# Block-local attention with a squared-ReLU network behind it: the normalisation on VectorE, block means by DMA, and twenty unread products on TensorE

## The chip, the cores and the metric

The kernel runs on one core of a Trainium2 chip. The metric is the device time of one execution in microseconds (us). The core's engines are TensorE (PE, with its weight loads as PEld), VectorE (DVE), ScalarE (ACT), GpSimd (POOL) and SyncE (SP, which here issues every DMA).

## The reference

Attention with B = 4, H = 8, S = 768, D = 64: each query sees the keys closer than 16 positions and, beside them, 24 block keys (the maximum of k over 32 positions, with log 32 added to their scores) whose values are the means of v over the same blocks. The result goes through a network of 512 to 2048 to 512 with a squared ReLU, without bias.

```python
k_sum = k.reshape(B, H, nb, block, D).max(axis=3)
v_sum = v.reshape(B, H, nb, block, D).mean(axis=3)
scores_s = scale * einsum('bhsd,bhnd->bhsn', q, k_sum) + log(block)
scores_l_m = where(|i - j| < window, scale * q @ k.T, -1e9)
a = softmax(concat([scores_l_m, scores_s]))
x = a @ concat([v, v_sum])
out = maximum(x @ w_in, 0) ** 2 @ w_out
```

All in float32 (the weights come as float64).

## The kernel before

**Attention.** The 3072 queries are 48 groups of 64 (group g = 12 b + w), all 8 heads of a group at once. A group's keys are 24 block keys and the 94 around it, 118 in all. The steps of a group, with the task names of the planner: QL loads q; LV loads the local rows of v to partitions 24 to 119 of the group's v tile (line 449, 96 rows of 2 KB), LS puts the 24 rows of block means ahead of them (line 452 a DMA, line 455 a copy on POOL for the first EARLY = 8 groups); S makes the scores (486), X the negated maxima (557, 561), E four exponentials with their sums on ACT (573), R the reciprocals (585, 586), N the product that normalises, on POOL (592), T the transpose (604 on PE for the first eight groups, 621 on DVE with a trip through HBM for the others), A its copy (611), V the product with v (648), XH and XL the high part and the rest of the result (700, 703). For the first eight groups XH is on DVE, for the others, which go in pairs, on ACT. The masks of the first eight groups are added by PE with a second product in S. For groups from 8 on a masking instruction M on DVE (541) does that.

**Per batch.** KL loads k in four pieces of 384 KB and KM takes block maxima on DVE (361). FV loads v in six pieces of 256 KB (405), VM makes means of them on PE (415, three tasks), VS copies the result from PSUM to the tile vs (427, on ACT). KC, a copy on POOL (496), moves the block keys ahead of the next group's local keys in the tile kb, so it has to come between two groups' scores.

**Network.** Six units of 512 tokens (eight groups), 16 slices f of 128 hidden columns. FI makes h = x w_in (813; twelve products of 512 columns: high by high, high by rest, rest by high), RL, SQ, GH, GL (822, 824 or 828, 830, 833) make the square and its two parts, FO adds to the four token blocks of o (843, again twelve products). In the first unit the slices 0 and 1 are split into halves a and b of four groups: h_0a, h_1a, h_0b, h_1b, and their FO likewise. During the first unit the weights are still being converted: WL loads half a slice (747, 512 KB), WM, WH on ACT (750, 764), WR, WJ, WW on DVE (753, 759, 767). PC copies o out (881).

**Order.** The program's order on each engine is the planner's. A task has an engine, a cost, a key (its due time), what it must follow, buffers that it takes, and for a load its size and an earliest time `begin`. `Plan.order()` plays the tasks through with these costs, starts on each free engine the ready task with the lowest key, and the instructions are written out in the order of the starts. So costs, keys, the load rate DMA_RATE and the list FIRST set the order on all engines, but no time on the chip: there each engine takes its list in order and waits by semaphores. SP issues its DMAs in order too.

## Time and profile before

| | |
|---|---|
| median of 3 runs | 635.62 us (635.41 to 636.62) |
| profiled execution | 635.87 us, its span 634.2 us |
| PE busy | 613.0 us, 97% of the span |
| DVE, ACT, POOL busy | 299.6, 268.7, 78.1 us |
| DMA, mean over the span | 116 GB/s |

The span runs from the first to the last instruction, so 1.7 us of the profiled execution lie outside of it. Busy time counts an engine's instructions, without issue and waits. In views of waits, idle time stands beside what ended it. A timeline row may hold several like instructions, with one start and their time together.

### The profile page before, as it was taken

How to read it: one execution, taken by the hardware profiler on the slowest of the kernel's cores; microseconds unless marked ns; L12 is line 12 of the kernel's file. 1: busy time of each engine (PE TensorE's matmuls, PEld its weight loads, DVE VectorE, ACT ScalarE, POOL GpSimd, SP SyncE). 2: the span in 40 equal slices, each digit the busy share in tenths (PEclk: the TensorE clock that was granted, in tenths of full speed). 3: DMA queues.
4: the chain of work that ended last, by engine and by line, in shares of the span. 5: the costliest groups of instructions: out<-in, count | busy, mean ns of one | idle time of the engine just before them, and what ended most of it. 6: DMA issues, size and time to landing. Idle time of an engine off the chain costs nothing.

```text
span 634.2 us, 11015 instructions
## 1 busy us (share of the span) xinstructions
PE 613.0 (97%) x4216; PEld 489.4 (77%) x4216; DVE 299.6 (47%) x517; ACT 268.7 (42%) x709; POOL 78.1 (12%) x140
## 2 busy tenths in 40 slices
PE   4779999999999999999999999999999999999997
PEld 3568788778777778777878778778788788888885
DVE  3798979633433433533543644534444432322221
ACT  1888778626544444332432523414343322222221
POOL 4731101101110110101210101201011010000000
PEclk9999999999999999999999999999999999999999
DMA  8998986244324832232415543133323020100001
GB/s 273 257 310 253 357 313 199 91 108 133 92 60 95 280 86 98 67 84 68 104 48 165 171 132 90 48 85 87 103 72 98 16 67 0 68 0 1 1 1 66
DMA packets 55448, 73.65 MB, mean 116 GB/s; under 512 B 6476, under 2 KB 33100, under 8 KB 55396
## 3 DMA queue, kind: packets, MB, share of 16 engines
q1 hardware_dynamic: 55396, 72.95, 39.0%
q8 instruction: 33, 0.54, 0.4%
q14 instruction: 19, 0.16, 0.1%
HBM read 55.56 MB, written 16.78 MB: 114 GB/s over the span
## 4 chain that ended last, share of the span: by engine, by line
PE 92%; DMA 7%; SPq 0%; DVE 0%; ACT 0%; issue 0%; DVEq 0%
PE o L843 42%; PE h L813 42%; PE x L648 3%; PE att L486 3%; DMA qvpa_lent<-qW 3%; DMA raw<-wW 2%; DMA q<-qW 1%; PE vps L415 1%; SPq L358 0%; PE h_0b L813 0%; PE h_1b L813 0%; DVE os L881 0%; ACT os L881 0%; DVE xl L703 0%; SPq L442 0%
## 5 line engine op out<-in xcount | busy, mean ns | idle before, releaser
L813 PE MATMUL h<-xh,w 128*128 128x512 f32 x752 | 236.9, 396 | 0.0
L843 PE MATMUL o<-w,gh 128*128 128x512 f32 x752 | 196.1, 395 | 1.4 <-DVE os L881 0.8
L843 PEld LDWEIGHTS o<-w,gh 128*128 128x128 f32 x752 | 139.7, 188 | 36.6 <-issue 2.7
L813 PEld LDWEIGHTS h<-xh,w 128*128 128x128 f32 x752 | 140.7, 188 | 33.8 <-issue 0.8
L813 PE MATMUL h<-xl,w 128*128 128x512 f32 x376 | 148.8, 396 | 0.0
L822 ACT ACTIVATE r<-h 128x512 f32<-128x512 f32 x94 | 56.2, 598 | 205.9 <-PE h L813 205.6
L833 DVE TENSOR_TENSOR gl<-r,gh 128x512 fp32r<-128x512 f32 x94 | 66.6, 709 | 101.6 <-ACT gh L830 65.5
L828 DVE TENSOR_TENSOR r<-r 128x512 f32<-128x512 f32 x64 | 45.2, 706 | 139.8 <-ACT r L822 139.7
L843 PE MATMUL o<-w,gl 128*128 128x512 f32 x376 | 106.4, 391 | 0.0
L813 PEld LDWEIGHTS h<-xl,w 128*128 128x128 f32 x376 | 70.6, 188 | 16.9
L843 PEld LDWEIGHTS o<-w,gl 128*128 128x128 f32 x376 | 70.6, 188 | 15.7
L830 ACT CAST gh<-r 128x512 fp32r<-128x512 f32 x94 | 58.3, 620 | 54.1 <-DVE r L828 27.8
L573 ACT ACTIVATE p<-p,nm 128x118 f32<-128x118 f32 x160 | 60.9, 383 | 30.8 <-DVE nm L557 30.7
L592 POOL TENSOR_TENSOR p<-p,nm 128x472 f32<-128x472 f32 x40 | 42.6, 1064 | 114.3 <-DVE nm L586 91.5
L496 POOL COPY kb<-kb 128x96 f32<-128x96 f32 x44 | 16.2, 368 | 306.1 <-PE att L486 282.7
L541 DVE SCALAR_TENSOR_TENSOR p<-att,mask 128x472 f32<-128x472 f32 x38 | 23.5, 644 | 27.8 <-PE att L486 27.8
L621 DVE STREAM_TRANSPOSE a<-p 128x512 f32<-128x512 f32 x40 | 28.3, 707 | 10.4 <-POOL p L592 9.0
L573 ACT ACTIVATION_READ_ACCUMULATOR p<-p,nm 128x1 f32 x160 | 30.0, 187 | 0.0
L557 DVE TENSOR_REDUCE nm<-p 128x4 f32<-128x472 f32 x40 | 25.0, 634 | 0.2
L486 PE MATMUL att<-kb,q 64*64 64x118 f32 x608 | 24.1, 274 | 0.0
L700 ACT CAST xh<-x 128x512 fp32r<-128x512 f32 x20 | 11.6, 582 | 28.6 <-PE x L648 28.6
L759 DVE SCALAR_TENSOR_TENSOR t<-t,raw 128x1024 uint32<-128x1024 uint32 (+1 forms) x19 | 21.8, 1148 | 3.5 <-ACT t L750 3.1
(104 smaller groups left out, 370.9 us busy)
## 6 DMA issues: line engine op xcount, KB each, us to landing
raw<-wW SPq DMA_DIRECT2D x32, 512.0 KB, 6.5
turn<-a SPq DMA_DIRECT2D x160, 64.0 KB, 1.8
a<-turn SPq DMA_DIRECT2D x40, 256.0 KB, 2.7
...
```

What stands on the lines that cost most here:

```text
L486: nc.tensor.matmul(score_tile(g)[c * TQ : (c + 1) * TQ, j, :], lhsT=q_bufs[g].tile[rows, p, :] if term else unscale[rows, :], rhs=kb[rows, ...
L541: nc.vector.scalar_tensor_tensor(out=pr.tile[:, js, :KEYS], in0=score_tile(g)[:, js], scalar=SCALE, in1=mask_of(g)[0].unsqueeze(1).broadca ...
L557: nc.vector.tensor_reduce(out=m, in_=score_tile(g)[:, js] if by_pe else pr.tile[:, js, :KEYS], op=ALU.max, axis=AX.X, negate=True)
L573: nc.scalar.activation(x, score_tile(g)[:, p] if by_pe else x, AF.Exp, bias=nm.tile[:, p : p + 1], scale=SCALE if by_pe else 1.0, accum_ou ...
L592: nc.gpsimd.tensor_tensor(out=x, in0=x, in1=nm.tile[:, 2 * NPAIR :].unsqueeze(2).broadcast_to([P, NPAIR, KEYS]), op=ALU.mult)
L621: nc.vector.transpose(out=a.tile.rearrange("p (j n r) -> p j n r", j=NSQ, n=NPAIR), in_=pr.tile.rearrange("p n (j c) -> p j n c", c=SQ),)
L813: nc.tensor.matmul(cut(h), lhsT=lhs.tile[:, k * P : (k + 1) * P], rhs=rhs[:, k, c0 : c0 + n], start=(i == 0), stop=(i == 3 * KT - 1),)
L822: t2 = add(f"RL{name}", "ACT", act, lambda: nc.scalar.activation(cut(r), cut(h), AF.Relu), due + 3, [t1], take=[r], use=[h])
L828: lambda: nc.vector.tensor_tensor(out=cut(r), in0=cut(r), in1=cut(r), op=ALU.mult), due + 4, [t2], use=[r],
L830: t4 = add(f"GH{name}", "ACT", act, lambda: nc.scalar.copy(out=cut(gh), in_=cut(r)), due + 5, [t3], take=[gh], use=[r])
L833: lambda: nc.vector.tensor_tensor(out=cut(gl), in0=cut(r), in1=cut(gh).bitcast(F32), op=ALU.subtract),
L843: nc.tensor.matmul(o_of(o, t), lhsT=terms[i][0].tile[:, (t - t0) * P : (t - t0 + 1) * P], rhs=terms[i][1].tile, start=(first and i == 0), ...
```

## The change

Line numbers in the diff are those of the changed kernel, which has 1033 lines against 981.

1. N, the normalising product, goes from POOL to DVE for all 48 groups.
2. XH of the first eight groups goes from DVE to ACT, VS of the first batch from ACT to DVE.
3. LS is a DMA for groups from 2 on (before: from 8 on). Two POOL copies are left.
4. LV of the first EARLY + NV = 11 groups reads a new input vF, filled on the host with the same rows of v in place and zeros elsewhere: 128 rows of 2 KB from partition 0, where 96 (or 94) rows went before.
5. Twenty products of the identity with itself (float32, 128 by 128) go into h buffers that nobody reads. They have the last priority on PE: the planner puts one wherever PE would pause. The planner's places are 11 before the first scores, 7 between the two halves of group 0's scores, one behind the first means and one behind the first transpose.
6. The planner's numbers: DMA_RATE, T0 (due time of the first network slice), the due times B0, B1 of groups 4 to 7, FIRST, the earliest `begin` of all other loads (16 instead of 8), and nearly all costs. Hence every engine's order is another.

```diff
-    HOP, DMA_LATENCY, DMA_RATE = 0.12, 1.9, 300e3
+    HOP, DMA_LATENCY, DMA_RATE = 0.12, 1.9, 370e3
...
-    T0, SLOW, STEP, LEAD = 33.0, 6.6, 6.0, 1.5
-    A0, A1, B0, B1 = 14.0, 2.2, 31.0, 2.6
+    T0, SLOW, STEP, LEAD = 29.0, 6.6, 6.0, 1.5
+    A0, A1, B0, B1 = 14.0, 2.2, 23.0, 2.2
...
-        "QL0 KL0_0 KL0_1 KL0_2 KL0_3 QL1 QL2 FV0_0 FV0_1 FV0_2 FV0_3 FV0_4 FV0_5 QL3 LV0 LV1 QL4 WL0_0 LV2 QL5 LV3 "
-        "QL6 LV4 QL7 LV5 WL0_1 LV6 LV7 WL1_0"
+        "QL0 KL0_0 KL0_1 KL0_2 KL0_3 QL1 QL2 FV0_0 FV0_1 FV0_2 FV0_3 FV0_4 FV0_5 QL3 LV0 LV1 QL4 LV2 QL5 LV3 "
+        "QL6 QL7 LV4 LV5 WL0_0 LV6 LV7"
...
+    def warm(i):
+        x = h_buf(f"warm{i}", P)
+
+        def mm():
+            nc.tensor.matmul(x.tile, lhsT=ident, rhs=ident, start=True, stop=True)
+
+        add(f"Y{i}", "PE", 0.42 if i < COLD else 0.22, mm, 1000 + i, [t_ident], take=[x])
+
+    for i in range(WARM):
+        warm(i)
...
-                nc.scalar.copy(out=vs.tile[:, c * P : (c + 1) * P], in_=out_ps.tile[c * SQ : c * SQ + NB, :P])
+                copy(out=vs.tile[:, c * P : (c + 1) * P], in_=out_ps.tile[c * SQ : c * SQ + NB, :P])
+
+        copy = nc.scalar.copy if b else nc.vector.tensor_copy
...
         def load_v():
+            if g < vF.shape[0]:
+
+                nc.sync.dma_start(out=vv.tile, in_=vF[g])
+                return
...
-            if not early:
-                lv.append(add(f"LS{g}", "SP", 0.45, load_s, due - 19, ts + lv, use=[vv, vs_bufs[b]], size=4 * NB * DM))
+            if g >= COPIED:
+                key = FIRST_LS + g if early else due - 19
+                lv.append(add(f"LS{g}", "SP", 0.45, load_s, key, ts + lv, use=[vv, vs_bufs[b]], size=4 * NB * DM))
...
-            nc.gpsimd.tensor_tensor(
+            nc.vector.tensor_tensor(
                 out=x, in0=x, in1=nm.tile[:, 2 * NPAIR :].unsqueeze(2).broadcast_to([P, NPAIR, KEYS]), op=ALU.mult
             )
...
-            (nc.vector.tensor_copy if n == 1 else nc.scalar.copy)(out=by_group(xh), in_=x_all())
+            (nc.vector.tensor_copy if g < HIGH_DVE else nc.scalar.copy)(out=by_group(xh), in_=x_all())
...
-            t.begin = max(t.begin, 8.0)
+            t.begin = max(t.begin, 16.0)
```

COPIED is 2, WARM 20, HIGH_DVE 0. A branch with ONE_EXP = 0 is never taken.

Three places of the order follow. In them, a number behind a name counts buffers, nm holds a group's maxima and sums, qvpa_lent and p are the tiles that hold its exponentials, raw, t and w are steps of a weight's conversion.

On DVE, at groups 3 and 4 of the first stage, there stood before (XH is line 700, XL 703):

```order
L557 TENSOR_REDUCE nm_394<-s_362 128x4
L561 TENSOR_SCALAR nm_394<-nm_394 128x4
L700 CAST xh<-att 128x4x64
L585 TENSOR_SCALAR nm_341<-nm_341 128x4
L586 RECIPROCAL nm_341<-nm_341 128x4
L703 TENSOR_TENSOR xl<-att,xh 128x4x64
L759 SCALAR_TENSOR_TENSOR t_0_405<-t_0_405,raw_0_172 128x512
```

Behind each reciprocal DVE went on without an N, since that was POOL's. With the change DVE has, at groups 4 to 6 (N is line 638):

```order
L798 TENSOR_SCALAR raw_0_276<-raw_0_276 128x512
L638 TENSOR_TENSOR qvpa_lent<-qvpa_lent,nm_411 128x4x118
L583 TENSOR_REDUCE nm_503<-s_464 128x4
L587 TENSOR_SCALAR nm_503<-nm_503 128x4
L631 TENSOR_SCALAR nm_453<-nm_453 128x4
L632 RECIPROCAL nm_453<-nm_453 128x4
L804 SCALAR_TENSOR_TENSOR t_0_508<-t_0_508,raw_0_276 128x512
L638 TENSOR_TENSOR qvpa_lent<-qvpa_lent,nm_453 128x4x118
```

Each group's N moved in between the group's reciprocals and the maxima of the group two later, and XH is gone from the list.

On PE, at slice 4 of the first unit, there stood before (415 is VM; gh_2 and gl_2 are the inputs of the FO of slice 2):

```order
L813 MATMUL h_4_886<-xl,w_860 128x512
L486 MATMUL att<-kb,q_281 64x118 x8
L648 MATMUL x_908<-a_729,v_75 64x64 x8
L648 MATMUL x_908<-a_791,v_76 64x64 x8
L486 MATMUL att<-kb,q_603 64x118 x8
L415 MATMUL vps_955<-fv_0_863,means 24x128 x8
L843 MATMUL o_0_709<-w_2_828,gh_2_866 128x512 x4
L843 MATMUL o_1_830<-w_2_828,gh_2_866 128x512 x4
L843 MATMUL o_0_709<-w_2_828,gl_2_882 128x512 x2
L843 MATMUL o_1_830<-w_2_828,gl_2_882 128x512 x2
L415 MATMUL vps_955<-fv_2_884,means 24x128 x8
L813 MATMUL h_5_1009<-xh,w_905 128x512 x2
```

FO stood two slices behind FI here. With the change PE has at this place (434 is VM, 888 is FO):

```order
L858 MATMUL h_4_987<-xl,w_908 128x512
L434 MATMUL vps_1017<-fv_0_935,means 24x128 x8
L888 MATMUL o_0_798<-w_844,gh_3_943 128x512 x4
L888 MATMUL o_1_864<-w_844,gh_3_943 128x512 x4
L888 MATMUL o_0_798<-w_844,gl_3_979 128x512 x2
L888 MATMUL o_1_864<-w_844,gl_3_979 128x512 x2
L858 MATMUL h_5_1065<-xh,w_940 128x512 x2
```

Behind the FI of slice 4 now comes the FO of slice 3: FO follows its FI one slice closer. The second and third VM both moved behind the FI of slice 5 (one stood ahead of it), so one more FO comes ahead of them.

On SP, at the loads of the second batch, there stood before (405 is FV, 358 is KL, 449 is LV):

```order
L405 DMA fv_0_863<-vS 128x512
L747 DMA raw_876<-wW 128x512 x2
L405 DMA fv_2_884<-vS 128x512 x2
L405 DMA fv_4_948<-vS 128x512 x2
L747 DMA raw_953<-wW 128x512
L442 DMA q_966<-qW 128x256
L449 DMA v_75<-vS 64x512
L449 DMA v_75<-vS 30x512
L358 DMA kb<-kT 128x768 x4
```

All FV came ahead of the loads of k. With the change SP has at this place (424 is FV, 377 is KL, 473 is LV):

```order
L424 DMA fv_0_935<-vS 128x512 x2
L424 DMA fv_2_985<-vS 128x512
L462 DMA q_1001<-qW 128x256
L473 DMA v_75<-vS 64x512
L473 DMA v_75<-vS 30x512
L377 DMA kb<-kT 128x768 x4
L424 DMA fv_2_985<-vS 128x512
L462 DMA q_1029<-qW 128x256
L424 DMA fv_4_1047<-vS 128x512 x2
L473 DMA v_76<-vS 96x512
```

The last three of the six FV moved behind the batch's four loads of k.

## Rows read from the trace of the kernel before

**Rows 1.** Waits of PE over the whole span: engine, line, releaser: us, times, longest.
```profile
PE s L486 <- DVE kb L361: 7.2, 3, 5.5
...
PE s L486 <- POOL kb L496: 0.6, 1, 0.6
```

**Rows 2.** Windows: length, busy us (x instructions) by engine, clock, DMA share, GB/s.
```profile
12.00:26.00 14.00, 12.45 (x272) 9.26 (x264) 8.75 (x25) 10.30 (x49) 8.50 (x18) 1.00 1.07 242
26.00:50.50 24.50, 18.48 (x253) 15.31 (x254) 23.89 (x54) 20.87 (x69) 11.59 (x16) 1.00 1.01 305
50.50:54.00 3.50, 3.50 (x16) 2.81 (x16) 3.50 (x7) 2.28 (x5) 0.00 (x0) 1.00 0.49 146
54.00:100.00 46.00, 46.00 (x347) 36.11 (x346) 40.03 (x52) 35.45 (x69) 2.77 (x5) 1.00 0.93 313
13.00:28.00 15.00, 12.79 (x293) 9.75 (x289) 9.95 (x29) 11.60 (x54) 9.89 (x17) 1.00 1.07 233
```

**Rows 3.** Timeline of PE: start us, us, instruction, idle before it and releaser.
```profile
10.76 0.46 PE L486 MATMUL s<-kb,qvpa_lent 64*64 64x118 f32 x2 [0.40 <-DVE kb L361]
...
13.19 0.62 PE L486 MATMUL s<-mask,unscale 64*64 64x118 f32 x8
...
15.39 0.38 PE L486 MATMUL s<-mask,unscale 64*64 64x118 f32 x8
...
46.25 0.39 PE L813 MATMUL h_0b<-xl,w 128*128 128x256 f32 x1 [1.05 <-DVE xl L703]
...
50.34 0.63 PE L813 MATMUL h<-xh,w 128*128 128x512 f32 x2
...
70.92 0.64 PE L415 MATMUL vps<-fv,means 128*24 128x128 f32 x16
...
74.36 0.62 PE L813 MATMUL h<-xh,w 128*128 128x512 f32 x2
...
77.16 2.02 PE L843 MATMUL o<-w,gh 128*128 128x512 f32 x8
```

**Rows 4.** Timeline of DVE, same columns.
```profile
20.77 0.43 DVE L753 TENSOR_SCALAR raw<-raw 128x512 uint32<-128x512 uint32 x1 [1.02 <-DMA raw<-wW]
...
21.40 0.39 DVE L700 CAST xh<-att 128x256 fp32r<-128x256 f32 x1
...
24.38 1.44 DVE L759 SCALAR_TENSOR_TENSOR t<-t,raw 128x512 uint32<-128x512 uint32 x1
...
34.72 0.66 DVE L759 SCALAR_TENSOR_TENSOR t<-t,raw 128x512 uint32<-128x512 uint32 x1
...
39.05 1.22 DVE L759 SCALAR_TENSOR_TENSOR t<-t,raw 128x512 uint32<-128x512 uint32 x1
...
45.81 0.38 DVE L703 TENSOR_TENSOR xl<-att,xh 128x256 fp32r<-128x256 f32 x1
...
76.37 0.91 DVE L833 TENSOR_TENSOR gl<-r,gh 128x512 fp32r<-128x512 f32 x1
```

**Rows 5.** Timeline of POOL, same columns.
```profile
1.88 0.29 POOL masks.py:199 TENSOR_SCALAR_AFFINE_SELECT ident<-ident 128x128 f32<-128x128 f32 x1
...
15.95 0.97 POOL L592 TENSOR_TENSOR qvpa_lent<-qvpa_lent,nm 128x472 f32<-128x472 f32 x1 [1.31 <-DVE nm L586]
...
18.56 1.15 POOL L455 COPY qvpa_lent<-vs 24x512 f32<-24x512 f32 x2
...
29.11 0.72 POOL L496 COPY kb<-kb 128x96 f32<-128x96 f32 x1
```

**Rows 6.** Timeline of ACT, same columns.
```profile
16.96 1.05 ACT L427 COPY vs<-vps 24x128 f32<-24x128 f32 x4
```

**Rows 7.** The page's costliest groups, line 541: xcount, busy us, mean ns.
```profile
L541 DVE SCALAR_TENSOR_TENSOR p<-att,mask 128x472 f32<-128x472 f32 x38 | 23.5, 644 | 27.8 <-PE att L486 27.8
```

**Rows 8.** Loads of line 405 in 50 to 75 us: first and last start, landing.
```profile
L405 SPq DMA_DIRECT2D fv<-vS x6: 334/424/611, 55.6 to 62.3; - x6
...
DMA to landing us min/median/max: 7.0/7.0/7.0
```

More of the change, by code (lines that the diff above doesn't have):

```diff
@@ L36 @@
 NV = 3
+COPIED = 2
+FIRST_LS = -180
+WARM, COLD = 20, 12
+HIGH_DVE = 0
+ONE_EXP = 0
 NPE = 8
@@ L385, in make_means @@
             )
-    t_means = add("means", "POOL", 1.8, make_means, -88)
+    t_means = add("means", "POOL", 1.0, make_means, -88)
     def batch_v(b):
@@ L426, in gather @@
             for c in range(NSQ):
-                nc.scalar.copy(out=vs.tile[:, c * P : (c + 1) * P], in_=out_ps.tile[c * SQ : c * SQ + NB, :P])
-        t_VS[b] = [add(f"VS{b}", "ACT", 1.1, gather, key + 7, [last], take=[vs], use=[out_ps])]
+                copy(out=vs.tile[:, c * P : (c + 1) * P], in_=out_ps.tile[c * SQ : c * SQ + NB, :P])
+        copy = nc.scalar.copy if b else nc.vector.tensor_copy
+        t_VS[b] = [add(f"VS{b}", "ACT" if b else "DVE", 1.1, gather, key + 7, [last], take=[vs], use=[out_ps])]
     t_QL, s_bufs = {}, {}
@@ L458, in loads @@
             add(f"LV{g}", "SP", 0.45, load_v, due - 20, behind=lq if early else None, take=[] if early else [vv],
-                use=[vv] if early else [], size=4 * LOC * DM, begin=due - 36)
+                use=[vv] if early else [], size=4 * (P if g < vF.shape[0] else LOC) * DM, begin=due - 36)
         ]
@@ L614, in turned @@
                 )
-            t_A[g] = add(f"A{g}", "ACT", 0.6, turned, due - 8.5, [t_T[g]], take=[] if early else [a], use=[at_ps] + [a] * early)
+            t_A[g] = add(f"A{g}", "ACT", 0.47, turned, due - 8.5, [t_T[g]], take=[] if early else [a], use=[at_ps] + [a] * early)
         else:
@@ L705, in low @@
             )
-        g = both[-1]
-        t_h = add(f"XH{g}", "DVE" if n == 1 else "ACT", 0.13 + 0.24 * n, high, due + 0.5, [t_v], use=[x_ps])
-        t_l = add(f"XL{g}", "DVE", 0.15 + 0.27 * n, low, due + 1, [t_h], use=[x_ps])
+        t_h = add(f"XH{g}", "DVE" if g < HIGH_DVE else "ACT", (0.334 if n == 1 else 0.48), high, due + 0.5, [t_v], use=[x_ps])
+        t_l = add(f"XL{g}", "DVE", 0.06 + 0.27 * n, low, due + 1, [t_h], use=[x_ps])
         for g in both:
@@ L880, in put @@
         t1 = add(
-            f"PC{u}_{t}", "ACT" if k else "DVE", 0.62 if k else 0.7, lambda: copy(out=part(), in_=o_tile()), due + 0.6, [t6],
+            f"PC{u}_{t}", "ACT" if k else "DVE", 0.48 if k else 0.6, lambda: copy(out=part(), in_=o_tile()), due + 0.6, [t6],
             take=[] if k else [x], use=[o] + [x] * k, behind=t_PC[-1] if k else None,
@@ L958 @@
     qW = np.ascontiguousarray(qd).reshape(B * (S // TQ), 2 * D, H // 2, TQ)
+    vS = np.ascontiguousarray(v.transpose(0, 2, 1, 3)).reshape(B, S, H * D)
+    vF = np.zeros((EARLY + NV, P, H * D), v.dtype)
+    for g in range(EARLY + NV):
+        k0 = first_key(g, S)
+        vF[g, S // BLOCK : S // BLOCK + LOC] = vS[0, k0 : k0 + LOC]
     w_in, w_out = inputs["moe_w_in"], inputs["moe_w_out"]
```

59 lines of the change are left out of this document (39 added, 20 removed).

## The prediction

> **What bounds the kernel now.** I read the waits of PE first, then windows, then the timelines of the stretch that has waits. PE's first wait is for the block maxima of k, 7.2 us in three pieces, the longest of them ahead of the first scores [rows 1]. From 50.34 us on, where the first product over a full unit starts [rows 3], PE has practically no pause: busy 3.50 of 3.50 us, then 46.00 of 46.00 [rows 2]. So the time is the end of the first stage plus a tail in which only products count, and the change leaves the products of that tail alone. It can gain by starting the tail earlier, and lose by opening gaps in it.
>
> The first stage has three parts. Up to about 11 us PE waits for k: the second half of group 0's scores starts at 10.76 us, behind the last maximum [rows 3]. From 12 to 26 us DVE is busy 8.75 of 14 us, with idle time before single steps (1.02 us at 20.77) [rows 2, 4]. From 26 to 50.5 us DVE is busy 23.89 of 24.50, against 18.48 on PE and 20.87 on ACT [rows 2]: here DVE's list sets the pace. At its end PE waits 1.05 us for the XL of group 7, which DVE starts at 45.81 and needs 0.38 for [rows 3, 4]. So DVE's list up to this XL at 46.2 us is the path. DMA is no spare resource either: its share is 1.01 to 1.07 up to 50.5 us and 0.93 from 54 to 100 [rows 2].
>
> **The change, part by part.** The sum is made against the profiled execution, 635.87 us, 0.25 above the median 635.62. It is made on DVE from 20.8 us, where DVE last idles for long, to the XL of group 7.
>
> *N on DVE.* No row shows it. The nearest is the masking instruction of the same shape on DVE, 0.644 us [rows 7]; the high end is the 0.91 of line 833 at 76.37 (512 columns and two inputs) [rows 4]. I take 0.64. Eight N come ahead of that XL. By the order three of them (groups 0 to 2) and VS come so early that the idle 5.25 us of 12 to 26 us hold them: 3 x 0.64, and VS at most ACT's 1.05 [rows 6], 3.0 in all. The other five count: **+3.2**.
>
> *XH to ACT.* Eight casts of 0.39 to 0.42 us leave DVE [rows 4]: **-3.3**. ACT gets as much, loses VS (1.05), and by its order does about 2 us of conversions later, so its list up to the last XH keeps its length. It had 3.6 us idle in the window, which covers it; without that cover each XH would put up to 0.4 us on the path.
>
> *Work put off.* Ahead of the XL of group 7 DVE no longer has one join and one rest of a weight (0.66 and about the same), one set of maxima (0.63), one transpose (0.7) and one half gl (0.4): **-3.1**. It comes later, ahead of the tail's FO.
>
> *POOL leaves.* A join on DVE takes 0.66 us alone (34.72) but 1.44 at 24.38 and 1.22 at 39.05, each beside a POOL copy or an N [rows 4, 5]. Six DVE instructions of that stretch are stretched so, these two the first and the last, by 0.4 to 0.8 us: 3.7 together. N (0.97 each on POOL) and six of the eight LS (18.56: two in 1.15) are what ran beside them [rows 5]. If those go, so does the excess: **-3.7**; the other end is 0.
>
> The sum on DVE is 3.2 - 3.3 - 3.1 - 3.7 = -6.9. But the first FO half now stands behind h_0b and h_1b, not ahead of them. Twelve products take 2.80 us (from 74.36 to 77.16 [rows 3]), the half 1.4, so the tail starts 6.9 - 1.4 = **5.5 us earlier**.
>
> [...] POOL's copy of the block keys took 0.72 us beside DVE at 29.11 [rows 5], and PE waited 0.6 for one [rows 1]. [...]
>
> *Unread products.* Low and high rates of PE show in a set of score products: 0.62 us at 13.19, 0.38 at 15.39 [rows 3]. Eleven products at no more than 0.62, from the identity's end at 2.2 us [rows 5], end by 9.0. They may hold the first half of group 0's scores, but what follows waits for the last maximum until 10.7 anyhow: cost 0. If that cover were gone, 3.5 us. If PE is at the high rate sooner, eight sets of groups 1 and 2 save 8 x 0.24 = 1.9 us at most; the third VM behind them waits for loads, and DVE's idle time has just been given to N and VS. I take 0, with 1.9 as the gain's end.
>
> *Loads.* vF adds 11 x 64 KB and LS six more DMAs of 48 KB, 1.0 MB. In 13 to 28 us, where loads of 96 rows are under way, 233 GB/s go through, and 242 to 313 elsewhere [rows 2]: 4.3 us of transfers at the low rate. Up to 100 us DMA has room for 3.5 x 0.51 + 46 x 0.07 = 5.0 us [rows 2], so I take 0 for the first stage, where v lies ahead of need.
>
> *What is late next.* Two things in the tail. First, the means of batch 1: the last of the FV was issued at 62.3 and took 7.0 us, 69.3, and its VM ran at 70.92 [rows 8, 3]: 1.6 us to spare. The tail comes 5.5 earlier, and the VM stands one FO (2.8) later in it. If the loads come no sooner, PE waits 5.5 - 1.6 - 2.8 = **1.1**. The ends are 0 and 7.6 (four loads of k and three smaller, 2.0 MB, now ahead of the last three FV, are 6.5 us at 313 GB/s); I take 1.1, nearer to the row in which the same total was moved by that time. Second, FO one slice closer to FI leaves a slice's gl the time of an FO and an FI, 5.6 us. Slice 5 needed 6.4: its FI ended at 70.9, its gl ended at 77.28 behind k's maxima [rows 3, 4]. That is 0.8 us of wait; ACT and DVE have full lists in that window (35.45 and 40.03 of 46 [rows 2], and the work put off comes on top), so I count two such: **1.6**, between 0 and 5.
>
> Sum: -5.5 + 1.1 + 1.6 = -2.8, **633.1 us**.
>
> **The rivals.**
> - *Nothing is given back.* FV and gl are in time, as all was in the tail before; against it speaks that 1.6 us were to spare for 5.5. Then 635.87 - 5.5 = 630.4.
> - *The excess isn't POOL's.* Not each overlap with POOL shows a stretch (a join at 34.72 ran at 0.66 just ahead of an N). Then the stage gains 5.5 - 3.7 = 1.8, FV is in time, one gl is late: -1.0, 634.9.
> - *N holds the copies.* Seven copies of block keys lie between groups 0 and 7. Half of 7 x 0.64 on PE's path would be 2.2: -0.6, 635.3. For it speaks PE's wait of 0.6, against it that POOL now has little else ahead of a copy.
> - *Slower: the transfers set the pace.* The 1.0 MB more at 233 GB/s make all behind them 4.3 us later, and the last FV of batch 1 come in their new place behind k. PE's wait at the third VM, near 65 us, is then 1.1 + 4.3 = 5.4, and the sum -5.5 + 5.4 + 1.6 = +1.5: 637.4. It is slower than before from a wait of 3.9 us on. For it: share 1.01 to 1.07 up to 50.5 us. Against it: 5.0 us of room, and rows of 128 partitions in place of 96, whose loads ran beside the lowest rate.
>
> **How the numbers follow.** The forecast gets 0.38 (its own range 631.5 to 634.6), nothing given back 0.17, excess not POOL's 0.17, N holds the copies 0.08, transfers 0.20. Under 0.2%, 1.3 us, a measurement can't be told from no change, so faster is under 634.35. That is nearly all of the forecast (0.34), all of the first rival and a fourth of the second: 0.55. The rest of the second, most of the third and parts of the forecast and of the last make "same" 0.25, and the last leaves 0.20 for slower. The range goes from 629.8, a little beyond the first rival for the unread products' gain, to 637.6, just beyond the last.
>
> **What would show it.** In the changed profile: N on DVE at 0.64 us, joins in the first stage at 0.66, XL of group 7 done near 39 us and the first full-unit product near 45 (before 50.34); then waits of PE of about 1.1 us for VM of batch 1 and 1.6 for gh or gl between 54 and 100 us, and none later. I am wrong if that product starts after 48 us, if joins stay at 1.2 to 1.4, if PE waits more than 4 us for VM or FO, or if the products of the tail themselves take another time.

## The result, and the profile after

The changed kernel takes 638.51 us (median of 13 runs, 637.01 to 640.46), the kernel before in the same comparison 636.62 (13 runs, 635.28 to 638.79): a ratio of **1.0032 [1.0018, 1.0045]**, slower by 2 us. The forecast was 633.1 and faster. The profiled execution is the slowest of the 13: 640.46 us, span 638.7 against 634.2. These 4.5 us are more than the 2 us between the medians; they can be laid out on PE from the rows of the two profiles:

| step | us |
|---|---|
| first product over a full unit, 50.34 [rows 3] to 46.18 | -4.2 |
| waits of PE for the loads of v that VM makes means of | +4.2 |
| products of FO, FI, V and VM that take longer | +3.8 |
| wait for a copy of block keys | +0.5 |
| end: wait for PC inside the last unit -0.8, from the last product to the end 3.9 to 5.0 | +0.3 |
| sum | +4.6 |

First the windows of the changed kernel (length, busy us by engine, clock, DMA share, GB/s):

```profile
12.00:26.00 14.00, 11.34 (x297) 9.05 (x288) 11.74 (x38) 10.48 (x52) 3.01 (x8) 1.00 0.91 302
26.00:50.50 24.50, 21.87 (x258) 18.50 (x253) 22.82 (x51) 22.88 (x70) 0.94 (x5) 1.00 0.85 297
54.00:100.00 46.00, 41.68 (x313) 31.48 (x312) 37.50 (x52) 30.35 (x62) 2.45 (x3) 0.93 0.86 283
70.00:75.00 5.00, 1.09 (x20) 0.35 (x23) 4.97 (x9) 1.16 (x2) 0.00 (x0) 0.89 1.05 330
75.00:80.00 5.00, 5.00 (x19) 3.65 (x20) 3.47 (x6) 2.20 (x5) 0.00 (x0) 0.50 1.01 353
```

Up to 50.5 us all went as meant: PE does 21.87 us of work in the second window where it did 18.48 [rows 2], POOL is out of it (0.94), and more bytes pass in 12 to 26 us (302 GB/s for 242). The loss stands in the third row: in 54 to 100 us PE is busy 41.68 of 46, where before it had no pause [rows 2], at a mean granted clock of 0.93. The last two rows say where: PE works 1.09 of 5 us, and in the next 5 the granted clock is 0.50.

The timeline of PE in the changed kernel shows both ends, the gain at the top:

```profile
40.71 0.39 PE L858 MATMUL h_0b<-xl,w 128*128 128x256 f32 x1 [0.16 <-DVE xl L749]
...
46.18 0.63 PE L858 MATMUL h<-xh,w 128*128 128x512 f32 x2
...
69.18 0.42 PE L434 MATMUL vps<-fv,means 128*24 128x128 f32 x8
72.72 0.42 PE L434 MATMUL vps<-fv,means 128*24 128x128 f32 x8 [3.12 <-DMA fv<-vS]
74.23 1.37 PE L434 MATMUL vps<-fv,means 128*24 128x128 f32 x16 [1.10 <-DMA fv<-vS]
75.53 3.78 PE L888 MATMUL o<-w,gh 128*128 128x512 f32 x8
79.12 1.84 PE L888 MATMUL o<-w,gl 128*128 128x512 f32 x4
...
83.59 2.00 PE L888 MATMUL o<-w,gh 128*128 128x512 f32 x8
85.44 1.07 PE L888 MATMUL o<-w,gl 128*128 128x512 f32 x4
```

The wait for XL of group 7 was 1.05 us [rows 3] and is 0.16. Then the second and third VM wait 3.12 and 1.10 us for loads, and the FO behind them takes from 75.53 to 80.79, the start of the next product: 5.3 us, where the FO at 83.59 takes 2.8. So in this profile the pause is paid twice, once as a wait and once as slow products behind it. All products behind the first full-unit one, summed by line, first before and then after (times, busy us, mean ns, idle time ahead):

```profile
L843 PE MATMUL o<-w,gh 128*128 128x512 f32 x752 | 196.1, 395 | 1.4 <-DVE os L881 0.8 <-ACT os L881 0.6
L843 PE MATMUL o<-w,gl 128*128 128x512 f32 x376 | 106.4, 391 | 0.0
...
L415 PE MATMUL vps<-fv,means 128*24 128x128 f32 x144 | 5.3, 276 | 0.0
```

```profile
L888 PE MATMUL o<-w,gh 128*128 128x512 f32 x752 | 197.6, 398 | 0.6 <-ACT os L926 0.6
L888 PE MATMUL o<-w,gl 128*128 128x512 f32 x376 | 107.2, 393 | 0.0
...
L434 PE MATMUL vps<-fv,means 128*24 128x128 f32 x144 | 6.2, 292 | 4.3 <-DMA fv<-vS 4.2
```

The counts are the same, the time is not: 1.5 + 0.8 + 0.9 us more, nearly all of it in that one stretch. With 0.3 each on FI and V this is the +3.8 of the table.

On DVE, N costs what the masking instruction did [rows 7], and joins are no longer stretched (before 1.44 and 1.22 [rows 4]); two steps wait for a weight's load, 1.0 us in all, of which this is the longer:

```profile
25.74 0.69 DVE L804 SCALAR_TENSOR_TENSOR t<-t,raw 128x512 uint32<-128x512 uint32 x1 [0.17 <-ACT t L795]
26.35 0.65 DVE L638 TENSOR_TENSOR qvpa_lent<-qvpa_lent,nm 128x472 f32<-128x472 f32 x1
27.83 0.43 DVE L798 TENSOR_SCALAR raw<-raw 128x512 uint32<-128x512 uint32 x1 [0.83 <-DMA raw<-wW]
...
40.26 0.39 DVE L749 TENSOR_TENSOR xl<-att,xh 128x256 fp32r<-128x256 f32 x1
```

Why the loads were late is read from SP, first what it waited for in 45 to 75 us, then its timeline:

```profile
SPq L684 <- DMA turn<-a: 7.5, 3, 4.2
SPq L424 <- DVE w L812: 2.3, 1, 2.3
```

```profile
50.24 1.84 SPq L678 DMA_DIRECT2D turn<-a  x4
55.88 0.35 SPq L684 DMA_DIRECT2D a<-turn  x1
56.36 0.83 SPq L792 DMA_DIRECT2D raw<-wW  x2
57.27 3.50 SPq L424 DMA_DIRECT2D fv<-vS  x3
...
62.68 1.78 SPq L377 DMA_DIRECT2D kb<-kT  x4
64.51 0.59 SPq L424 DMA_DIRECT2D fv<-vS  x1
...
66.25 1.54 SPq L424 DMA_DIRECT2D fv<-vS  x2
```

Line 678 stores the transposed exponentials of a group to HBM, line 684 reads them back. In this order a pair's reads stand right behind its own stores, so SP stands still until the stores have landed, and with it every load behind: 7.5 us here, 2.9 in the same window before. The first FV leaves at 57.27 us, 1.7 later than before, although the stage ended 4.2 earlier. Then the loads of k and small ones go out ahead of the last three FV. The last two leave at 66.25 us and after, where before it was 62.3 [rows 8]. While SP stands the DMA engines have room: their share is 0.60 in 46 to 60 us, where before it was 0.81. From 60 to 70 us it is 0.95.

### The profile page after: what moved, and what is told of

It is laid out like the page before. It is cut to its first block, busy times and chain, and to the rows that moved or that the text cites. A ratio compares the mean times of both kernels' runs of the same rounds, so it can differ in the third digit from the quotient of the medians.

```text
span 638.7 us, 11007 instructions
## 1 busy us (share of the span) xinstructions
PE 619.4 (97%) x4256; PEld 496.2 (78%) x4256; DVE 316.3 (50%) x561; ACT 270.3 (42%) x713; POOL 24.7 (4%) x86
## 4 chain that ended last, share of the span: by engine, by line
PE 88%; DMA 6%; DVE 2%; SPq 1%; ACT 1%; issue 1%; POOL 0%; DVEq 0%; ACTq 0%; POOLq 0%
PE o L888 41%; PE h L858 40%; PE att L511 3%; PE x L694 3%; DMA raw<-wW 2%; DMA fv<-vS 1%; DMA qvpa_lent<-vs 1%; DMA kb<-kT 1%; DMA turn<-a 1%; PE vps L434 1%; PE s L511 1%; SPq L377 0%; DVE w L812 0%; PE att L694 0%; SPq L462 0%
## 5 line engine op out<-in xcount | busy, mean ns | idle before, releaser
L878 DVE TENSOR_TENSOR gl<-r,gh 128x512 fp32r<-128x512 f32 x94 | 64.7, 690 | 99.5 <-ACT gh L875 62.0
L638 DVE TENSOR_TENSOR p<-p,nm 128x472 f32<-128x472 f32 x40 | 25.9, 648 | 1.0
L694 PE MATMUL x<-a,v 118*64 118x64 f32 x640 | 23.3, 225 | 0.0
L694 PEld LDWEIGHTS x<-a,v 118*64 118x64 f32 x640 | 20.4, 138 | 3.4 <-issue 3.3
```

Source lines behind the costliest of these rows:

```text
L638: nc.vector.tensor_tensor(out=x, in0=x, in1=nm.tile[:, 2 * NPAIR :].unsqueeze(2).broadcast_to([P, NPAIR, KEYS]), op=ALU.mult)
L694: nc.tensor.matmul(x_of(i)[h % 2 * D : (h % 2 + 1) * D, h // 2, :], lhsT=v_bufs[g].tile[:KEYS, h * D : (h + 1) * D], rhs=av[:KEYS, 2 * c : ...
L878: lambda: nc.vector.tensor_tensor(out=cut(gl), in0=cut(r), in1=cut(gh).bitcast(F32), op=ALU.subtract),
```

## The experiments

All kernels keep the order of the changed kernel but for the moves shown. Each ratio is to the kernel before, timed beside it on the same chip (medians of 636.67 to 637.17 us there). A ratio can differ from the quotient of the two medians by up to 0.002 (e16), and differences of less than some 0.3% between two experiments lie within their intervals, so the profiles carry as much of the argument as the ratios.

### The pause in the tail

**e0_after**, the changed kernel again, to have it beside the experiments.

> The changed kernel again, as the base of the three beside it on the same chip. All theories: 1.003 of the kernel before; the first full-unit product near 46.2 us against 50.3, waits of PE for the loads of batch 1's v of about 4 us near 70 us, and a granted clock under 1 in the 10 us behind them.

638.79 us, 1.0042 [1.0021, 1.0063]. The profile has the waits for means (3.4 us in three) and the low clock behind them (0.57 in 74 to 82 us). It also has an early pause that the first profile had not: DVE waits 2.01 us for the load of a weight at 29.22, and PE stands 3.1 us. Behind that pause the granted clock falls, as it does in the tail:

```profile
30.00:34.00 4.00, 2.90 (x24) 2.53 (x24) 3.19 (x12) 2.56 (x10) 0.00 (x0) 0.55 0.98 345
34.00:38.00 4.00, 4.00 (x55) 3.14 (x55) 2.61 (x6) 3.14 (x7) 0.27 (x1) 0.60 1.02 361
```

The first full-unit product comes at 49.01 instead of 46.18, so in this execution 2.8 of the first stage's 4.2 us are lost. SP stands at other entries too: 3.7 us at the reads behind their stores, 4.0 at a store that waits for DVE, 3.7 at FV for a weight's buffer.

**e1_fv_first**: all FV of batch 1 ahead of the loads of k, as before the change.

```diff
-        for t in plan.order():
+        tasks = plan.order()
...
+        move_behind("QL13 LV11 KL1_0 KL1_1 KL1_2 KL1_3 QL14".split(), "FV1_5")
+        move_behind("KM1_0 KM1_1 KM1_2 KM1_3".split(), "T11")
+        for t in tasks:
```

> The four loads of batch 1's k, three small loads and the maxima of k are moved behind batch 1's last loads of v and behind group 11's transpose; nothing else. Theory 1 (the gain of 4.2 us of the first stage is lost to the 4.2 us wait for v and to 2.5 us of products at the low clock behind it): the wait falls under 1.5 us, the clock stays 1.00, the time falls by 5 to 7 us to 0.993 to 0.996 of before. Theory 2 (DVE and ACT are full there, and would hold PE a little later anyway): PE waits for gh, gl or weights instead, and the ratio stays at 1.000 or above.

639.28 us, 1.0054 [1.0034, 1.0075]. No wait for means is left, and nothing is won. Waits of PE, then its timeline:

```profile
PE o L888 <- ACT gh L875: 4.2, 2, 3.3
```

```profile
85.83 3.46 PE L888 MATMUL o<-w,gh 128*128 128x512 f32 x8 [3.26 <-ACT gh L875]
```

ACT's list has weight conversions ahead of that gh, whose loads now come later: ACT stands 6.3 us ahead of one (line 795, starting at 79.46). The wait has the same 4.2 us in total and only another name, and products are slow behind it again (3.46 us for eight, where 2.0 is usual; the granted clock is 0.66 in 85 to 90 us). So the loads of k ahead of FV are one cause of the wait for means, but to move them only makes other loads late.

**e2_fill**: nineteen products more that nobody reads, put into PE's two pauses, at the second and third VM of batch 1.

```diff
+                    for _ in range({(2, 1): 14, (4, 0): 5}.get((i, k), 0) if b == 1 else 0):
+                        nc.tensor.matmul(out_ps.tile[:, P : 2 * P], lhsT=ident, rhs=ident, start=False, stop=False)
```

> Nineteen more unread 128x128 products on PE, 14 where it waits for the fourth v load of batch 1 and 5 ahead of the fifth: the wait is filled, not shortened. Theory 1: the clock stays 1.00 behind it and the FO that took 5.3 us takes 2.8, so the time falls by 2 to 3 us, to 0.998 to 1.000 of before. Rival (the low clock costs nothing, since DVE, ACT or DMA would hold PE at that place anyway): the time stays at 1.003, and waits for gl, gh or weights appear behind the FO.

637.49 us, 1.0018 [1.0002, 1.0035]. The loads are as late, but PE is not idle, and the FO behind is at the full rate. Timeline of PE, then a window:

```profile
73.92 1.38 PE L434 MATMUL vps<-ident 128*128 128x128 f32 x10
75.23 0.64 PE L436 MATMUL vps<-fv,means 128*24 128x128 f32 x16
75.80 2.11 PE L890 MATMUL o<-w,gh 128*128 128x512 f32 x8
```

```profile
75.00:80.00 5.00, 5.00 (x37) 3.96 (x36) 3.68 (x6) 2.20 (x5) 0.00 (x0) 1.00 1.04 383
```

The clock is 1.00 where it was 0.50, and this FO takes 2.8 us for 5.3. Over the whole execution the mean granted clock is 0.996 to 1.000 in all 12 runs, in e0's 0.988 to 0.996. So the slow products behind the pause are caused by the pause. They are worth 2.5 us in the profile; the ratio falls by some 1.5 us (1.0042 to 1.0018), with intervals that overlap.

**e8_trip**: SP's two reads of the first transposed pair stand two and four loads later, so that SP need not wait for the stores.

```diff
...
+        move_behind(["TR8"], "WL1_6")
+        move_behind(["TR9"], "FV1_1")
```

> SP's order alone: the weights of slices 6 and 7 and the first two v loads of batch 1 are issued between the stores and the read of groups 8's and 9's transpose trip through HBM, where SP stood waiting (7.5 us) with DMA half idle from 46 to 60 us. Theory 3 (the tail is late because SP stood still behind those trips, so that later loads crowd from 65 to 90 us): DMA's share from 46 to 60 us rises from 0.50 to 0.65 to 0.8 or more, the last v loads land 3 us or more sooner, PE's wait for them falls from 4 us to under 2, the ratio from 1.003 to 1.004 down to 0.996 to 1.000. Rival (buffers or the loads' own rate hold them, not SP): the loads wait for their buffers instead, wait of PE and ratio stay.

636.73 us, 1.0004 [0.9986, 1.0023]: no longer slower than before. Windows of e8 and, for the same stretch, of the changed kernel:

```profile
46.00:54.00 8.00, 8.00 (x36) 6.47 (x35) 7.96 (x15) 7.77 (x12) 0.00 (x0) 1.00 0.83 270
```

```profile
46.00:54.00 8.00, 8.00 (x36) 6.47 (x35) 7.96 (x14) 7.97 (x16) 0.00 (x0) 1.00 0.57 188
```

SP's wait for the stores falls from 7.5 to 0.8 us, 270 GB/s pass in place of 188, and PE's wait for means falls from 4.2 to 1.5. Over 46 to 60 us, the stretch that the expectation named, the share rises from 0.60 only to 0.71. So SP's order makes the loads late, while the DMA engines have room. The rest of the wait stays; SP now stands 6.2 us at FV for a buffer that a weight's conversion still holds. The move has a price too: PE waits 1.3 us for the read that comes later, and 0.9 for a gh.

**e9_trip_fv**, e8 and e1 together:

> The order of the run before it, and batch 1's loads of k and the maxima of k put behind batch 1's v as in the first reordering (where the wait moved to gh of slice 6, 3.3 us). Theory 3: with the loads sooner, neither wait is left (each under 1 us), the clock stays 1.00 from 46 us on, and the ratio is 0.992 to 0.997. Rival (the transfers as a whole are too many up to 90 us): a wait of 2 us or more for gh, gl or weights stays, ratio 1.000 or above.

638.92 us, 1.0038 [1.0015, 1.0061]. PE waits for gh again (4.5 us in two), and the DMA share in 60 to 65 us is only 0.34, since SP stands 9.8 us at FV for buffers. Putting FV first gains nothing with either order of the trip.

**e12_lent** gives the FV of batch 1 the tiles of the last two weights, which are not yet in use; **e11_trip_lent** is that and e8.

```diff
...
+        for i, place, k in ((0, "w15", 0), (2, "w15", 2), (4, "w14", 0)):
+            if not k:
+                x = buf(place, 1, (P, 4 * DM), F32, f"fv1_{place}")
+            named[f"FV1_{i}"].take = [x] * (not k)
+            for j, part in enumerate(later[1, i]):
+                part.buf, part.a, part.b = x, (k + j) * DM, (k + j + 1) * DM
```

> The changed kernel with only the borrowed tiles for batch 1's v loads, SP's order as it was. Theory 3: SP still stands at the trips (7.5 us) but no longer at the v loads (2.3 us), so PE's wait for v falls from 4 us to 1 to 3 us, the ratio to 0.999 to 1.002. If the buffers were all that mattered, it would be as good as the run with both; if the trips were, as the changed kernel.

637.09 us, 0.9996 [0.9977, 1.0014]. SP waits 7.7 us for the stores, as in the changed kernel, and PE 3.0 us for means.

> SP's order with the two trips as before (e8_trip), and batch 1's v loads go into two tiles that later hold the weights of slices 14 and 15, so that SP no longer waits for a conversion's buffer ahead of them (6.2 us in that run). Theory 3: the v loads land before 69 us, PE's waits for them (1.5 us) and for the trip's read (1.3 us) go, DMA is busier from 54 to 65 us, the ratio falls by another 0.003 to 0.006, to 0.994 to 0.998. Rival (the transfers as a whole are too many): the wait moves to gh, gl or weights between 70 and 100 us, and the ratio stays at 1.000 or above.

636.19 us, 0.9981 [0.9959, 1.0002]. SP waits 2.6 us for the stores and no more for a weight's buffer, the DMA share is 1.00 in 54 to 60 us and PE waits 1.1 us for means, with a granted clock of 1.00 in 70 to 80 us. From the first full-unit product to the end of the span its profile takes 586.7 us, the changed kernel's 592.5, e8's 588.9, e12's 589.9 and the kernel before 583.9. So most of the loss in the tail is mended, and each remedy alone took part of it. The median is below that of the kernel before, but the interval reaches 1.

### The parts of the change

One profile shows what a move does to the first stage only within limits. Eight profiles have the first stage of the changed kernel (its own two, e1, e2, e8, e9, e11, e12). The first full-unit product comes at 45.28 to 46.52 us in the three whose mean granted clock up to it is 1.00, at 45.96 to 47.52 in the four with 0.96, and at 49.01 in e0 with 0.93. So each of the following is to be held against a profile of like clock.

**e10_order**: all moves undone (N on POOL, XH on DVE, VS on ACT, LS by POOL copies, LV of 96 rows, no unread products), only the new order kept.

```diff
...
-            nc.vector.tensor_tensor(
+            nc.gpsimd.tensor_tensor(
...
-            (nc.vector.tensor_copy if g < HIGH_DVE else nc.scalar.copy)(out=by_group(xh), in_=x_all())
+            (nc.vector.tensor_copy if n == 1 else nc.scalar.copy)(out=by_group(xh), in_=x_all())
...
-        copy = nc.scalar.copy if b else nc.vector.tensor_copy
+        copy = nc.scalar.copy
...
+            if g < EARLY:
+                return copy_s()
...
-            if g < vF.shape[0]:
+            if g < 0:
...
+        tasks = [t for t in tasks if t.name[0] != "Y"]
```

> Only the order of the changed kernel is kept. N is back on POOL, XH of the first eight groups back on DVE, VS of batch 0 back on ACT, LS of groups 2 to 7 back on POOL, the v loads have 96 rows from vS again, and the twenty unread products are left out. Theory 4 (each of these moves alone is a zero sum, and the 4 us of the first stage come from the order, which takes fewer weights into it): the first full-unit product comes at 46 to 48 us, the ratio is 1.003 to 1.008. Rival (they come from the moves together): the product comes at 49 to 51 us.

644.37 us, 1.0109 [1.0090, 1.0129], the first full-unit product at 52.38 (clock 0.97), later than either theory had it. So the new order alone is worse than the old, and the moves together bring back 4 us of it (against e0, intervals apart). The parts, one at a time:

**e7_xh_dve**: XH of the first eight groups back on DVE (the second edit of e10).

> XH of the first eight groups goes back to DVE in the changed kernel, nothing else. If it is this move that makes room on DVE (eight casts of 0.4 us), the first full-unit product comes 2 to 4 us later than 46.2 and the ratio rises by 0.001 to 0.004. Rival (ACT's list is as full, so the move is a zero sum like N's): product and ratio stay within 1 us and 0.001.

641.81 us, 1.0076 [1.0050, 1.0103], the first full-unit product at 50.27, 4.1 later than in the changed kernel's first profile, but 1.3 later than in e0's, which has the same clock of 0.93. The ratio is up by 0.3%, with intervals that overlap. Of the moves undone alone (VS was not) this is the only one that puts the product outside the range of the eight profiles.

**e4_n_pool**: N back on POOL (the first edit of e10).

> N goes back to POOL at its place in the order, the rest as in the changed kernel. If the stretched joins were POOL's doing, joins of 1.2 to 1.4 us are back in the first stage, and the first full-unit product, at 46.2 to 49.0 in the changed kernel, comes 1 to 4 us later, the ratio rises by 0 to 0.004 (a part is taken up by the wait for v). Rival (moving N is a zero sum: DVE saves 0.64 us for each N and loses the like by stretch): the product within 1 us and the ratio within 0.001.

640.52 us, 1.0066 [1.0045, 1.0088], up by 0.0024 against e0 with intervals that overlap; the first full-unit product comes at 46.26, no later than 46.18. One instruction of DVE, two of POOL:

```profile
26.28 1.49 DVE L804 SCALAR_TENSOR_TENSOR t<-t,raw 128x512 uint32<-128x512 uint32 x1 [0.18 <-ACT t L795]
```

```profile
26.24 0.97 POOL L638 TENSOR_TENSOR qvpa_lent<-qvpa_lent,nm 128x472 f32<-128x472 f32 x1 [1.01 <-ACT t L795]
27.16 0.73 POOL L521 COPY kb<-kb 128x96 f32<-128x96 f32 x1
```

The join (line 804) is back at 1.49 us for 0.69, beside POOL's N, which began 0.04 us earlier; and POOL's copy of block keys behind it takes 0.73, where most take 0.27. N itself keeps its 0.97, and the join takes 0.8 more; by what mechanism, no run shows. Yet the end of the stage does not move in this profile (clock 1.00). Up to that product DVE is busy 32.18 us, in the changed kernel 34.52: its eight N take 5.3 us there, so more than half of that comes back as longer instructions. The rest goes into waits, for scores 4.7 us in 12 to 46 us in place of 2.7, and 1.2 for ACT. PE waits 2.3 us for copies of block keys here, in place of 0.5.

**e14_xh_n**, both undone:

> XH on DVE and N on POOL, both as before the change, the rest as changed. With all moves undone the first full-unit product came at 52.4 us, with N alone undone at 46.3. If DVE's list is the path and the two moves are one exchange (N for XH), this product comes between 48 and 51 us. Rival (the padded loads, the DMA of block means and the unread products bring the rest, the exchange nothing): 46 to 47.5 us.

641.47 us, 1.0072 [1.0049, 1.0094], product at 50.09 (clock 0.93): with XH on DVE, N on POOL or on DVE makes no difference that can be measured (1.0072 and 1.0076).

**e3_no_unread**, without the twenty unread products (the last edit of e10):

> The twenty unread products are left out, every engine's order else the same. Theory 1 (DVE's list sets the pace of the first stage, the products only raise the clock a little earlier): products run at the low rate up to about 14 us again, the first full-unit product moves by 0 to 1.5 us later, the ratio by 0 to +0.002. Rival (the eleven ahead of the scores hold them, since they end at 6.6 where scores began at 5.5): the first full-unit product comes 0.5 to 1 us earlier.

640.02 us, 1.0059 [1.0037, 1.0080], product at 46.35 (clock 1.00). Score products in e3, then in the changed kernel:

```profile
14.15 0.62 PE L511 MATMUL s<-mask,unscale 64*64 64x118 f32 x8
```

```profile
12.99 0.38 PE L511 MATMUL s<-mask,unscale 64*64 64x118 f32 x8
```

By the length of its products PE is at its low rate without them until about 15.5 us: a set takes 0.62 us up to 14.15 and 0.38 from 15.89 on. With them it is at the high rate from some 5.6 us on: an unread product takes 0.42 us up to there and 0.28 behind. The granted clock in 5 to 20 us is 1.00 in both, so here it does not show the rate. The end of the stage differs by 0.2 us, less than the profiles scatter, and the ratios by 1 us, within the intervals. So nothing shows that the products gain time, and nothing that they hold anything up.

**e5_v96**: LV of 96 rows again.

> The v loads of the first 11 groups have 96 rows from vS again, in the same places of the order. If loads of 96 rows are what made DMA slow in the first stage (233 GB/s from 13 to 28 us before, against 289 to 302 up to 26 us now), that stretch falls back to 240 GB/s or less, landings go from 5.6 to over 7 us, and the first full-unit product comes 1 us or more later. Rival (the number of bytes sets it): landings shorten, the product is no later.

640.73 us, 1.0059 [1.0037, 1.0081], product at 48.53 (clock 0.93, so no later than in e0). In 13 to 28 us 231 GB/s pass, as the low rate of [rows 2] had it, in the changed kernel 299. Part of that is the padding of vF, up to 0.7 of the 1.0 MB between them. But the DMA share is 0.96 for the smaller rate and 0.89 for the larger, and the loads take 6.1 us to land with 192 KB, 5.6 with 256 (the expectation had over 7). So the loads of 128 rows are faster; no gain in time shows.

**e6_ls_pool**: LS of groups 2 to 7 by POOL (the fourth edit of e10).

> The block means of groups 2 to 7 are copied by POOL again, at the same place of the order, instead of six DMAs of 48 KB. If these DMAs, issued from 17.8 to 28.4 us and landing some 2.6 us later, gate the products with v (PE waited up to 3.1 us at 28 to 31 us, with the clock at 0.50 behind it in one execution), that wait goes, the first full-unit product comes 1 to 2 us earlier and the ratio falls by 0 to 0.002. Rival (the copies stretch DVE's instructions as before): single joins of 1.1 us or more come back and the product is no earlier.

639.68 us, 1.0047 [1.0029, 1.0065], product at 46.13 (clock 1.00): the ratio is that of e0. In its profile DVE waits for no weight's load.

### What is left in the first stage

**e13_lent_more**: e11 with 14 unread products more, five between the two halves of group 0's scores and nine at the second and third VM of batch 1.

> The best of the runs so far (both trips, borrowed tiles) with 14 more unread products where PE still pauses: 5 between the halves of group 0's scores, 9 at batch 1's v. If the clock's falls behind pauses are what is left of the loss, the clock stays at 1.00 in more executions and the ratio goes from 0.998 to 0.994 to 0.997. Rival (the falls came by chance of the execution, or the products delay what follows): 0.998 or above.

636.61 us, 1.0002 [0.9984, 1.0019]. The mean granted clock is 0.997 to 1.000 in all 12 runs, e11's 0.993 to 1.000, and it isn't faster. So the clock is not all that is left. The timeline of DVE and that of PE in its profile:

```profile
29.93 0.43 DVE L802 TENSOR_SCALAR raw<-raw 128x512 uint32<-128x512 uint32 x1 [2.69 <-DMA raw<-wW]
```

```profile
31.82 0.69 PE L698 MATMUL att<-qvpa_lent 118*64 118x64 f32 x16 [3.77 <-issue]
```

DVE's first step of a weight (line 802, the rest WR0_1) stands ahead of the maxima of group 7 and holds them 2.69 us for its load, PE stands 3.77 us, the granted clock behind is 0.66 in 32 to 37 us, and the first full-unit product comes at 48.59.

**e15_lent_wr**: e11, that one step four places later on DVE.

```diff
...
+        move_behind(["WR0_1"], "M8")
```

> Built on the order with the two later reads of the trip and with the lent buffers (0.9981 [0.9959, 1.0002]); alone WR0_1, the DVE step that waited 0.8 to 2.7 us for a weight load in other runs while it stood ahead of the maxima of group 7, comes four DVE steps later. Theory: that wait at the head of DVE's list is what keeps the first stage long in many executions: no pause of PE over 1 us between 28 and 33 us, the first product over a full unit at 45.0 to 46.5 us, ratio 0.994 to 0.998. Rival: the load is late because the queue of transfers is, and whoever waits next (maxima, ACT's conversions, h_0b) takes the same time: product at 47 or later, ratio 0.998 or more.

635.70 us, 0.9976 [0.9953, 0.9999]. The interval ends just under 1, which is weak evidence for one of eighteen experiments. The profile, of an execution with a late load (637.77 us), shows the wait at the next step of the same kind:

```profile
30.94 0.43 DVE L799 TENSOR_SCALAR raw<-raw 128x512 uint32<-128x512 uint32 x1 [1.38 <-DMA raw<-wW]
```

```profile
33.84 1.09 PE L651 MATMUL t<-ident,qvpa_lent 128*128 128x128 f32 x4 [2.54 <-DVE qvpa_lent L639]
```

The first product over a full unit is at 48.44, so the expectation's sign (no pause at 28 to 33 us) didn't come: moving one step hands the wait to the next. The load itself is late.

**e16_lent_ls**: e11 with LS of groups 2 to 7 by POOL, six DMAs less on SP.

> Built on the same order with lent buffers; the block means of groups 2 to 7 go by POOL copies again, so SP has six DMAs of 48 KB less among the weight loads of the first stage. Theory: these DMAs delay the weight loads that stand behind them on SP, so without them DVE waits at most 0.5 us for raw, product at 45.0 to 46.5 us, ratio 0.994 to 0.998. Rival: POOL's copies lengthen DVE's joins again (1.2 us and more in place of 0.66) and give it back: product at 46.5 or later, ratio 0.998 to 1.003.

635.39 us, 0.9991 [0.9966, 1.0016]. DVE waits for no weight, PE makes no pause over 1.2 us from 26 us on, and the product comes at 46.53. Product and ratio are where the rival had them, but its mechanism isn't: the joins take 0.68 to 0.69 us. The ratio alone doesn't tell it from e11. SP shows what the six DMAs do. First its rows in the changed kernel, then in e16 (lines 476 LS, 792 and 795 WL):

```profile
17.80 1.67 SPq L476 DMA_DIRECT2D qvpa_lent<-vs  x2
...
20.54 2.13 SPq L476 DMA_DIRECT2D qvpa_lent<-vs  x2
...
23.48 1.86 SPq L792 DMA_DIRECT2D raw<-wW  x2
```

```profile
19.36 0.99 SPq L795 DMA_DIRECT2D raw<-wW  x2
```

With LS on SP the second weight load of that stretch leaves 4 us later. It leaves at 22.98 to 25.37 us in the fifteen profiles with LS by DMA, and at 19.24 to 19.38 in e6, e16 and e17 (in e10, which has loads of 96 rows besides, at 22.84).

**e17_both**: e15 and e16 together.

> The order with the two later reads of the trip, the lent buffers, WR0_1 four steps later on DVE, and the block means of groups 2 to 7 by POOL copies. Alone the last two gave 0.9976 [0.9953, 0.9999] and 0.9991 [0.9966, 1.0016]; in the first DVE still waited 1.4 us for another weight's load at 30.9 us, in the second it waited for none. Theory (the lateness of the weight loads is what is left, and six DMAs less bring them in time): no wait of DVE for raw over 0.5 us, first product over a full unit at 44.5 to 46.0 us, ratio 0.994 to 0.998. Rival (POOL's copies give back on DVE what the loads gain): product at 46.0 or later, ratio 0.998 or more.

634.64 us against 636.72, 0.9983 [0.9964, 1.0002]. The profiled execution is 633.53 us, span 631.7. A window, PE's wait for means, and its timeline:

```profile
54.00:100.00 46.00, 44.63 (x338) 34.41 (x337) 41.99 (x60) 35.66 (x74) 1.12 (x3) 1.00 0.83 278
```

```profile
PE vps L435 <- DMA fv_w<-vS: 1.0, 2, 0.6
```

```profile
45.69 0.63 PE L861 MATMUL h<-xh,w 128*128 128x512 f32 x2
```

No wait for a weight on DVE, a granted clock of 1.00, and a wait of 1.0 us in place of 4.2. In all four kernels of the new order whose LS go by POOL (e6, e10, e16, e17) the profile shows no wait of DVE for a weight's load between 20 and 46 us; of the fifteen profiles with LS by DMA twelve show one, 0.44 to 2.69 us (e1, e3 and e4 none). LS by POOL alone isn't enough for that: in the old order, with LS by POOL too, DVE waited 1.3 us. POOL's copies stretched no join here (0.68 to 0.69). Of the 4.7 us by which the product comes earlier than before, the span keeps 2.5. From that product on it is 2.2 us longer than before: 0.5 in waits of PE, 0.9 from the last product to the end, the rest in products of FI, V and VM. e17 and e15 are the best versions, e15 with an interval just below 1, e17 with the lowest median; their intervals don't tell them apart, nor from e11 and e16.

## Why the prediction was wrong

**The bound, right.** The end of the first stage and the tail's gaps decide the time, as said.

**The first stage, right in size.** Forecast 5.5 us, measured 4.2. XL of group 7 was to end near 39 us and ended at 40.26 + 0.39 = 40.65; the 1.3 us are the same in both. 1.0 of them is DVE's wait for weight loads (0.83 and 0.18), which "so I take 0 for the first stage" left out; that wait is 0 to 2.7 us over the profiles, and in e0 it was 2.0, with a stretch at low granted clock behind it (0.57 in 30 to 38 us) and 2.8 us less gain. N at 0.64 to 0.72, VS at 1.17 and joins at 0.66 to 0.69 are as priced. The terms N (+3.2) and "POOL leaves" (-3.7) nearly cancel in the sum, and e4's product at 46.26 against 46.18 doesn't speak against it; but DVE's busy time there is 2.3 us less, so N did lengthen DVE's list by that much, with 3.0 of its 5.3 us given back by shorter instructions. For XH (-3.3) e7 shows a loss when it goes back, 1.3 us against a profile of like clock. What the work put off gave by itself no run shows; the new order without the moves loses 2 us of the stage (e10). The rivals "the excess isn't POOL's" and "N holds the copies" fall with e4, whose join beside POOL's N takes 1.49 again, and with PE's wait for the copies, 0.5 us. Of the ten copies up to 33 us in the changed kernel nine take 0.27 us; the one that begins inside an N of DVE, at 23.92, takes 0.56. So no run shows the 2.2 us that "N holds the copies" put on PE's path.

**The step that failed: "What is late next".** The first term, 1.1 us for the wait at the means, was 4.2. It rested on "if the loads come no sooner", that is, on FV that leave at the time they left before. The last two left 4 to 5 us later. Part of that the prediction had seen, the loads of k ahead of them, and had put into its upper end of 7.6 instead of the sum; without them no wait for means is left (e1). The other part had no term: the waits of the queue that issues the loads. In the new order SP's list has reads right behind their own stores (7.5 us, before 2.9); e8 takes that away and the wait falls to 1.5. The rival "transfers set the pace" had the place (the third VM), nearly the size (5.4 for 4.2) and the sign, but not the mechanism: the share of the DMA engines was 0.57 to 0.65 in 46 to 60 us, not full, and came near 1 only behind that (0.95 in 60 to 70 us), when the late loads came together.

The second term of that step, 1.6 us for gh and gl, was 0 in the changed kernel: with FV late, gh had time. It comes back, at 0.9 to 4.5 us, in e8, e1 and e9, where FV comes sooner; in e11 and e15 to e17, where it comes sooner too, PE waits for neither.

**What had no term at all**: PE's rate behind a pause. "PE waits 1.1" was taken as costing 1.1. In the changed kernel a wait of 4.2 us cost 2.5 us more in the FO behind it, and e2 shows that a filled pause doesn't. With -4.2 + 4.2 most of the rest of the loss is this. Two of the prediction's own signs of being wrong came true: PE waited more than 4 us for VM, and the products of the tail took another time.

**The measure.** The 635.62 us of three runs, on which the sum stood, is at the favourable end of the kernel before: in the longer series its median is 637. Against a fixed 635.6 the loss would look larger than the 0.3% that it is.

**Unread products, right**: cost 0, and no gain that can be measured (e3), though the shorter products come 10 us sooner (at 5.6 us for 15.5).

Still open: what the six LS on SP are worth in time (SP's rows show that they make weight loads leave 4 us later, but the ratios of e6 and e16 show no gain without them), and which part of 1 to 2 us each move is worth in the median, since most experiments with one move undone lie within each other's intervals.

## What to carry to other kernels

A stage that ends 4 us earlier is worth 4 us only if the queue that issues the loads gets through its list 4 us earlier too: here its last loads of v left 4 to 5 us later instead. So read the list of the issuing queue in order like that of a compute engine: mark each entry that waits for something, above all a read that stands right behind the store that it reads, and ask what stands behind it. Price a pause of the tensor engine as the wait plus the slow products behind it, and look in the windows for the granted clock of the stretch that follows: here 4.2 us of waits, with 5 us at 0.50 behind them, cost 2.5 us more. Look for a load that is waited for at the head of a list of short steps: in e13 it held DVE's list for 2.69 us, and PE stood 3.77. Steps that depend on a transfer can go behind those that don't, but in e15, with one of them moved, the next one waited 1.38 us.

## What the runs showed of the chip

- The kernel before isn't free of the low clock either: its 29 runs beside e0 have a mean granted clock of 0.991 to 0.999, and the time goes with it: 633.8 to 635.1 us in the nine runs at 0.999, 637.5 to 638.2 in the five at 0.991. The changed kernel's lay at 0.993 to 0.997 in all 13 runs of the first comparison, e17's at 0.997 to 0.999 in 11 of 12. Beside e17 the four runs of the kernel before at 0.999 take 633.9 to 634.5 us, e17's six at 0.999 take 633.5 to 635.5. So at the same clock the two show no difference, and what separates their medians goes with the mean granted clock of the executions; which stretch lowers it in the kernel before, no profile shows.
- Pauses of PE were followed by slow products in several places: the granted clock was 0.50 in 75 to 80 us behind 3.12 and 1.10 us of waits for transfers, 0.55 in 30 to 34 behind 3.1 us (e0), 0.66 in 85 to 90 around a wait of 3.26 (e1), and 0.66 in 12 to 17 in e11, where PE had stood 1.65 us up to 11.55. Not every pause is: the changed kernel's first profile has one of 1.10 us before 11.09 and 1.00 behind it.
- Two executions of the same kernel can differ by one load: DVE's wait for it at 27 to 30 us was 0.83 us in one profile of the changed kernel and 2.01 in the other, the granted clock behind it 1.00 and 0.55 to 0.60, and the first full-unit product 46.18 and 49.01.
